# Three w_out loads and the loads of steps 6 and 7 change places in one DMA queue of an mLSTM + MLP kernel, with the conversion of w_out later and half of the key/query copies on VectorE

## The chip, the cores and the metric

The kernel runs on 1 core of one Trainium2 chip. Its time is the device time of one execution in microseconds (us). Before the change it is 527.63 us, the median of 3 runs (525.84 to 529.88). The profile is one further execution of 524.4 us, whose recorded span is 522.5 us; 1.9 us lie around the span. All times of day below are microseconds from the start of that span.

## The reference

Two blocks follow each other. The first is an mLSTM cell over 4 batches, 8 heads, 768 positions and head size 40:

```python
for t in range(S):
    m_new = np.maximum(f_gate[:, :, t] + m, i_gate[:, :, t])
    ...
    C = f_stab * C + i_stab * np.einsum('bhd,bhe->bhde', vt, kt)
    n = f_stab * n + i_stab * kt
    h_tilde = np.einsum('bhde,bhe->bhd', C, qt)
    denom = np.maximum(np.abs(np.einsum('bhd,bhd->bh', n, qt)), 1.0)
    y[:, :, t] = sigmoid(o_gate) * h_tilde / denom
```

Its result, seen as 3072 tokens of 320 values, goes through an MLP: `h = x @ w_in` (320 to 2048), `g = max(0.01*h, h)`, `out = g @ w_out` (2048 to 320). The two weight matrices arrive as 8-byte floats; everything is computed in fp32.

## The kernel before

**Tiling.** The 768 positions are 6 chunks of 128. A step is one chunk of one batch, so steps 0 to 3 are chunk 0, steps 4 to 7 chunk 1, and so on to step 23. The MLP of chunk g is a list of "ff units", which the main loop runs in the pass c = g + 1, and between these units it puts the attention work of chunk c ("cells"). So the pass c = 1 holds the MLP of chunk 0 and the attention of steps 4 to 7. In this pass 30 units remain, numbered i = 0 to 29 in the loop: i = 0 to 13 are the first product in half tiles (`half`, TensorE L790, ScalarE's activation at L798), i = 14 to 29 are the second product (`part`, TensorE L825): 14 to 17 need rows of w_out pieces 0 and 1, 18 to 21 pieces 2 and 3, 22 to 25 pieces 4 and 5, 26 to 29 pieces 6 and 7.

**Order.** The instructions of TensorE, VectorE, ScalarE and GpSimd stand in the order in which the program writes them. The loads are issued by SP, one queue in order; their places among each other come out of the scheduler, which sets an issue later when what it overwrites is still in use. In the built program every SP transfer also waits for the one eight places before it in the queue.

**A step of chunk 1** has these parts. Loads: `load` brings k into `kn` (L380) and v in four pieces into `S` (L383); `spread` brings the decay row into `w` (L437, two transfers from the kernel's own scratch `a_dr`); both together are `feed(s)`. `load_late(s, 1)` brings q into `rb` (L406), called from `ahead(s - 2)`; `load_late(s, 2)` the output gate. GpSimd adds the mask to w (L479), scales q into `y` (L517), k into `vu` (L508), and the state (L622). `u_split` turns k and q with 64 small matmuls into two PSUM banks (L564, "tk"), each of which then holds k of one half step and q of the other, and four copies bring them to `kqT` (L570). `u_parts` first splits the scaled q (L550 "tq", copies at L552), then makes scores and state update (L644 and L649, "sd"); ScalarE makes the exponentials of w (L488, eight per step, handed out between other work), VectorE multiplies them with the scores into `qn` (L654). `u_plain` makes the outputs (L695, "hN").

The cells of steps 4, 5, 6 and 7 stand behind fixed units: `u_parts` behind i = 2, 7, 12 and 18, `u_plain` behind i = 5, 10, 15 and 21. `u_split(s + 1)` comes right behind `u_plain(s)`.

**Weights.** Pieces of 8-byte floats are loaded by `load_weights` (w_in at L222, w_out at L229, eight w_out pieces of 640 KB) and converted by `narrow_weights`: ScalarE L243, ScalarE L245, VectorE L247, ScalarE L251, VectorE L253, VectorE L257. The generator `now` hands these six steps out, so many per unit: first the last two pieces of w_in (12 steps, done at i = 7 before and after the change), then w_out pieces 0 to 7 (48 steps).

Of the kernel before, what the change touches and what calls it, by code (L numbers as in the profile page):

```python
# [21 lines left out]
def kernel(  # L22
# [26 lines left out]
    nc = tc.nc  # L49
    B, H, S, D = q.shape  # L50
# [12 lines left out]
    SL = P // 2  # L63
# [30 lines left out]
    def load_fi(c):  # L94
        t = fi[c] = wk.tile([BH, 2, P], F32, name="fi")
        eng = nc.scalar if c < 3 else nc.sync
        eng.dma_start(t[:, 0, :], f_all[:, ts(c, P)])
        eng.dma_start(t[:, 1, :], i_all[:, ts(c, P)])
# [65 lines left out]
    QN = NF // 4  # L164
# [20 lines left out]
    def run_of(r, at):  # L185

        ks = SLOTS[r][at:]
        return ks[0], next((i for i in range(1, len(ks)) if ks[i] != ks[i - 1] + 2), len(ks))

    def load_weights(n, halves=(0, 1)):  # L190

        m = n - QN
        if n < QN:
            dst = w_in[:, n, :]
        else:
            dst = w_out[:, 2 * m : 2 * m + 2, :].rearrange("p a d -> p (a d)")
        to = dst
        if wide:
            if n < 2:
                at = NF * GT - 2 * WC * (n + 1)  # L200
                raw = acts_l[:, at : at + 2 * WC].bitcast(U64)
            elif n < QN:
                raw = raw_t[:, WC * (n - 2) : WC * (n - 1)]
            elif m < 2:
                raw = w_out[:].rearrange("p f d -> p (f d)")[:, (2 + m) * WC : (3 + m) * WC].bitcast(U64)
            else:
                at = (4, 0, 1, 2, 3, 4)[m - 2] * HW
                raw = raw_t[:, at : at + HW]
            raws[n] = (raw, dst)
            to = raw  # L210
        if n < QN:
            src = moe_w_in[:, n * QC : (n + 1) * QC].rearrange("(k p) (r c) -> r p k c", p=DP, r=2)
            by_slot = to.rearrange("p (k c) -> p k c", k=KC)
            by_half = to.rearrange("p (e k c) -> p e k c", e=2, c=P)
            for r in halves:
                at = 0
                while at < KC:
                    k0, many = run_of(r, at)
                    rows, ks = slice(DP * r, DP * (r + 1)), slice(k0, k0 + 2 * many - 1, 2)
                    eng = nc.gpsimd if r and n < 3 else nc.sync  # L220
                    if wide or n > 1:
                        eng.dma_start(by_slot[rows, at : at + many, :], src[r, :, ks, :])  # L222
                    else:
                        for e in range(2):
                            eng.dma_start(by_half[rows, e, at : at + many, :], src[r, :, ks, e * P : (e + 1) * P])
                    at += many
        else:
            rows = moe_w_out[2 * m * P : 2 * (m + 1) * P, :]
            nc.sync.dma_start(to.rearrange("p (a d) -> p a d", d=Dm), rows.rearrange("(a p) d -> p a d", p=P))  # L229
# [166 lines left out]
    def natural(s, i):  # L396

        t = rb_t[s % NR][:, i]
        return t[:, : H * D].rearrange("p (h d) -> p h d", d=D)
# [154 lines left out]
    def u_split(s):  # L554

        d = st[s]
        d["kqT"] = wk.tile([P, 2, PR * P], F32, name="kqT")
        src = (d["k"], natural(s, 1))
        bank = [psc.tile([P, H, SL], F32, name=f"tk{r}", tag="c") for r in range(2)]
        for h in range(H):  # L560
            for i in range(2):
                for u, toks, rows in subs(s):
                    out_rows = rows if i == 0 else slice(SL * u, SL * u + D)
                    nc.tensor.matmul(  # L564
                        bank[u][out_rows, h, :], lhsT=src[i][toks, h, :D], rhs=ident[toks, toks], start=True, stop=True,
                    )
        for i in range(2):
            for u, toks, rows in subs(s):
                out_rows = rows if i == 0 else slice(SL * u, SL * u + D)
                nc.scalar.copy(d["kqT"][rows, i].rearrange("p (h t) -> p h t", t=SL), bank[u][out_rows])  # L570

    def u_transpose(s, copy=nc.scalar.copy):
        d = st[s]
# [289 lines left out]
    def run(steps, n=None):  # L863

        for _ in range(H if n is None else n):
            next(steps, None)

    def ahead(s):

        if s < NS:  # L870
            if s < 2 * B:
                u_split(s)
            if s >= 2 * B:
                late[s] = 3
            lazy[s] = prep_exp(s)
            if s < 2 * B:
                prep_qs(s)
            else:
                prep_kq(s)
            if s + NR < NS:  # L880
                load_late(s + NR, 0)
                load_late(s + NR, 1)
                if s + NR >= 2 * B:
                    spread_q(s + NR)
            state_next(s, 0)
            prep_vu(s)
            if s + 1 <= 2 * B:
                prep_mask(s + 1)

    def feed(s):  # L890
        load(s)
        spread(s)
# [96 lines left out]
    with tc.manual_schedule(engines={E.PE, E.DVE, E.Activation, E.Pool}):  # L989
        ffs, part = first_chunk()  # L990
        for s in (B, B + 1):
            load_late(s, 1)
            feed(s)
            load_late(s, 2)
            load_weights(s - B + 2)
        for n in range(3):
            load_weights(QN + n)
        for s in (B + 2, B + 3):
            feed(s)


        ffs = ffs[2:]
        fetch = {5: (3, 4), 8: (5, 6), 15: (7,)}
        place = (2, 5, 7, 10, 12, 15, 16, 18, 21, 22, 24, 26, 28)
        late = {}
        masks = {0: (2, 3), 12: (4, 5)}
        pairs = (2, 2, 6, 6, 14, 14, 19, 19, 19)
        now = (None for n in range(2, QN + NF // 2) for _ in narrow_weights(n))
        for c in range(1, NB + 1):
            if c > 1:  # L1010
                ffs = ff_units(c - 1)
            cells = cell_units(c) if c < NB else []
            n_ff, n_c = len(ffs), len(cells)
            done = fed = 0
            waiting = []
            for i in range(n_ff):
                if c == 1:
                    run(now, (0, 0, 0, 3, 3, 0)[i] if i < 6 else 3 if i < 14 else 4)
                    for n in fetch.get(i, ()):
                        load_weights(QN + n)  # L1020
                for s, steps in lazy.items():
                    if s in late and late[s] > 0:
                        late[s] -= 1
                    else:
                        run(steps, 3)
                for n in masks.get(i, ()) if 1 < c < NB else ():
                    if c * B + n < NS:
                        prep_mask(c * B + n)
                ffs[i]()
                if c == 1 and i == 0:  # L1030
                    run(part)
                    prep_mask(B)
                    ahead(B)
                    load_fi(3)
                if c + 1 < NB:
                    if i == (1 if c == 1 else 0):
                        gates(c + 1)
                    if i == (3 if c == 1 else 2):
                        gates_exp(c + 1)
                upto = min(n_c, sum(p <= i for p in (place if c == 1 else pairs)))  # L1040
                while done < upto:
                    fn, s = cells[done]
                    fn(s)
                    done += 1
                    if fn is u_mix:
                        waiting.append(s)
                    if fn is u_plain and s < 2 * B - 1 or fn is u_parts and s == 2 * B - 1:
                        ahead(s + 1)
                    elif fn is u_mix:
                        ahead(s + 2)  # L1050
                    elif fn is u_plain:
                        prep_mask(s + 2)
                        ahead(s + 2)
                if i >= n_ff // 2 - 1:
                    for s in waiting:
                        gather_x(s)
                    waiting.clear()
                while fed < done:
                    fn, s = cells[fed]
                    fed += 1  # L1060
                    if fn in (u_mix, u_plain):
                        load_late(s + NR, 2)
                        if s + NL < NS:
                            feed(s + NL)
# [31 lines left out]
```

## Time and profile before

| | PE | DVE (VectorE) | ACT (ScalarE) | POOL (GpSimd) |
|---|---|---|---|---|
| busy us of the 522.5 us span | 509.1 | 205.3 | 187.6 | 106.9 |
| share of the span | 97% | 39% | 36% | 20% |

Time of the profiled execution: 524.4 us; its span: 522.5 us; mean granted TensorE clock 0.992. In the page, PE is TensorE's matmuls, SP the engine that issues the loads. Over the span the chain of work that ended last lies 89% on PE, 5% on SP's queue and 2% on transfers. From 90 us to the end of the last product TensorE is busy without a gap that the profile shows.

By lines, TensorE spends 216.5 us in the first product (L790) and 211.1 us in the second (L825). Of the waits of TensorE's matmuls the longest single one is the one for `rb<-in_q_dram` in L564: 2.9 us. The SP queue carries 56.31 MB in 163408 packets, most of them under 512 bytes.

### The profile page before, as it was taken

To read this page: it belongs to the slowest core of one execution; us is meant where nothing else is said; L and a number is where in the kernel's file an instruction comes from. 1 tells how busy PE (TensorE), PEld (TensorE's weight loads), DVE (VectorE), ACT (ScalarE), POOL (GpSimd) and SP (SyncE) were. 2 spreads that over 40 slices of the span, in tenths; PEclk is the share of its full clock that TensorE was granted. 3 is DMA by queue.
4 is the path that set the end of the run, shared out by engine and by line. 5 is a ranking of instruction groups with operands and counts; after the bars stand their busy time and mean duration, and the time that the engine had idled before them with its cause. 6 is when DMAs were issued, how large, how long until landed. Compare 5 with 4: busy or idle time off the path is not lost.

```text
span 522.5 us, 11302 instructions
## 1 busy us (share of the span) xinstructions
PE 509.1 (97%) x4507; PEld 331.1 (63%) x4507; DVE 205.3 (39%) x400; ACT 187.6 (36%) x477; POOL 106.9 (20%) x149
## 2 busy tenths in 40 slices
PE   8989987999999999999999999999999999999997
PEld 6878876777554677554677554677554677544674
DVE  6666453767048264048264038253037240000000
ACT  5559896858425122125112125112125100122100
POOL 4363313424015031016021016021013010000000
PEclk9889999999999999999999999999999999999999
DMA  9999875989646535665536665625532112000000
GB/s 122 137 206 156 180 188 145 220 196 169 159 92 135 127 80 148 141 140 125 123 93 155 139 140 116 134 82 157 136 77 71 44 40 87 14 0 1 13 13 25
DMA packets 164419, 59.12 MB, mean 113 GB/s; under 512 B 128432, under 2 KB 155632, under 8 KB 164368
## 3 DMA queue, kind: packets, MB, share of 16 engines
q1 hardware_dynamic: 163408, 56.31, 50.1%
q0 software_dynamic: 576, 1.97, 2.0%
q8 instruction: 35, 0.57, 0.5%
q10 hardware_dynamic: 384, 0.13, 0.1%
q14 instruction: 16, 0.13, 0.1%
HBM read 51.68 MB, written 6.70 MB: 112 GB/s over the span
## 4 chain that ended last, share of the span: by engine, by line
PE 89%; SPq 5%; DMA 2%; ACT 2%; issue 1%; DVE 1%; ACTq 0%; DVEq 0%
PE po L825 40%; PE ph L790 39%; SPq L378 3%; PE pT L725 3%; PE sd L644 3%; DMA acts<-in_moe_w_in_dram 1%; PE sd L649 1%; PE tk L564 1%; PE hN L695 1%; DMA rb<-in_q_dram 1%; PE tq L550 1%; SPq L383 0%; SPq L392 0%; ACT kqT L570 0%; PE tg L357 0%
## 5 line engine op out<-in xcount | busy, mean ns | idle before, releaser
L790 PE MATMUL ph<-xT,w_in 64*128 64x512 f32 (+1 forms) x1120 | 216.5, 537 | 3.5 <-ACT acts L798 1.9
L825 PE MATMUL po<-w_out,acts 128*128 128x320 f32 x768 | 211.1, 434 | 0.0
L825 PEld LDWEIGHTS po<-w_out,acts 128*128 128x128 f32 x768 | 144.5, 190 | 62.6 <-issue 3.8
L790 PEld LDWEIGHTS ph<-xT,w_in 64*128 64x128 f32 x1120 | 108.6, 189 | 97.5 <-issue 87.7
L798 ACT ACTIVATE acts<-ph 128x512 f32<-128x512 f32 (+1 forms) x112 | 53.6, 531 | 141.5 <-PE ph L790 141.5
L654 DVE TENSOR_TENSOR qn<-w,sd 64x512 f32<-64x512 f32 x40 | 27.4, 684 | 106.7 <-PE sd L649 58.6
L479 POOL TENSOR_TENSOR w<-w,i 128x512 f32<-128x512 f32 x20 | 27.3, 1375 | 126.0 <-DMA w<-a_dr 74.0
L622 POOL TENSOR_TENSOR S<-S,f 40x336 f32<-40x336 f32 x36 | 28.0, 779 | 102.1 <-PE pT L725 65.2
L488 ACT ACTIVATE w<-w,gT 128x64 f32<-128x64 f32 x160 | 41.2, 338 | 0.0
L833 ACT COPY y<-po 128x320 f32<-128x320 f32 x12 | 5.1, 422 | 83.2 <-PE po L825 83.2
L833 ACT COPY hn<-po 128x320 f32<-128x320 f32 x12 | 5.1, 425 | 75.7 <-PE po L825 75.7
L541 DVE TENSOR_TENSOR qn<-kqT,ea 64x512 f32<-64x512 f32 x32 | 26.9, 840 | 0.9
L732 DVE STREAM_TRANSPOSE hb<-pT 128x512 f32<-128x512 f32 x16 | 11.4, 714 | 39.2 <-PE pT L725 39.0
L739 POOL TENSOR_TENSOR xb<-xb,den 128x320 f32<-128x320 f32 x16 | 11.6, 727 | 67.1 <-DVE xb L736 67.1
L644 PEld LDWEIGHTS sd<-kqT 40*64 40x64 f32 x640 | 19.9, 135 | 6.1 <-issue 6.1
L644 PE MATMUL sd<-kqT 40*64 40x64 f32 x640 | 21.6, 220 | 0.0
L535 DVE STREAM_TRANSPOSE kqT<-rb 128x512 f32<-128x512 f32 x32 | 20.7, 686 | 1.2 <-DMA rb<-in_q_dram 1.1
L743 DVE STREAM_TRANSPOSE x<-xb 128x512 f32<-128x512 f32 x16 | 18.1, 1132 | 7.7 <-POOL xb L739 7.7
L649 PE MATMUL sd<-S,vu 64*40 64x42 f32 x576 | 20.2, 214 | 0.7 <-issue 0.7
L649 PEld LDWEIGHTS sd<-S,vu 64*40 64x40 f32 x576 | 18.6, 111 | 0.9 <-issue 0.9
L626 DVE TENSOR_TENSOR S<-S,sd 40x336 f32<-40x336 f32 x36 | 18.1, 503 | 1.0
L725 PEld LDWEIGHTS pT<-qn,S 128*64 128x64 f32 x512 | 15.6, 138 | 3.6 <-issue 3.5
(138 smaller groups left out, 348.9 us busy)
## 6 DMA issues: line engine op xcount, KB each, us to landing
w<-a_dr SPq DMA_DIRECT2D x40, 128.0 KB
rb<-in_k_dram SPq DMA_DIRECT2D x64, 80.0 KB
rb<-in_q_dram SPq DMA_DIRECT2D x64, 80.0 KB
rb<-in_o_gate_dram SPq DMA_DIRECT2D x64, 80.0 KB
ea<-a_dr SPq DMA_DIRECT2D x32, 128.0 KB
kn<-in_k_dram SPq DMA_DIRECT2D x24, 160.0 KB
raw<-in_moe_w_out_dram SPq DMA_DIRECT2D x6, 640.0 KB
S<-in_v_dram SPq DMA_DIRECT2D x80, 40.0 KB
```

The costliest lines, as they stand in the source:

```text
L479: nc.gpsimd.tensor_tensor(w, w, cm2.unsqueeze(1).to_broadcast([P, H, SL]), op=ALU.add)
L488: yield nc.scalar.activation(w[:, h, :], of, AF.Exp, bias=gT[c][:, 0, bh : bh + 1], scale=1.0)
L535: nc.vector.transpose(d["kqT"][:, i].rearrange("p (h t n) -> p h n t", n=TS, t=QW), raw_blocks(s, i, QW).rearrange("p (h n) d -> p h n d", ...
L541: nc.vector.tensor_tensor(mixed(s)[rows, 1 - r], d["kqT"][rows, 1].rearrange("p (h t) -> p h t", t=SL), d["ea"][rows], op=ALU.mult,)
L622: nc.gpsimd.tensor_tensor(new, old, g, op=ALU.mult)
L644: nc.tensor.matmul(bank[1 - u][toks, h, :], lhsT=kqT[rows, 0, ts(h, SL)], rhs=kqT[rows, 1, ts(h, SL)], start=True, stop=True,)
L649: nc.tensor.matmul(dC[u][:, h].rearrange("p k d -> p (k d)"), lhsT=d["ku"][toks, h], rhs=S_v[s % NL][toks, u, h, :, :V1], start=True, stop ...
L654: nc.vector.tensor_tensor(mixed(s)[toks, u], w[toks], bank[1 - u][toks], op=ALU.mult)
L725: nc.tensor.matmul(pT[DP * r : DP * (r + 1), j * P + u * SL : j * P + (u + 1) * SL], lhsT=S[:, u, h, :], rhs=m[:, u, h, :], start=True, st ...
L790: nc.tensor.matmul(ph[r][:, cols], lhsT=w_row(r, slot, j), rhs=xT[DP * r : DP * (r + 1), slot, cols], start=(slot == 0), stop=(slot == KC ...
L798: nc.scalar.activation(acts[:, f, cols], ph[r][:, cols], AF.Prelu, alpha=0.01)
L825: nc.tensor.matmul(po[n][:], lhsT=acts[:, f, ts(n, P)], rhs=w_out[:, f, :], start=(f == 0), stop=(f == NF - 1),)
```

## The change

```diff
@@ u_split
-                nc.scalar.copy(d["kqT"][rows, i].rearrange("p (h t) -> p h t", t=SL), bank[u][out_rows])
+                (nc.vector.tensor_copy if i else nc.scalar.copy)(
+                    d["kqT"][rows, i].rearrange("p (h t) -> p h t", t=SL), bank[u][out_rows],
+                )
@@ before the main loop
             load_weights(s - B + 2)
-        for n in range(3):
-            load_weights(QN + n)
-        for s in (B + 2, B + 3):
-            feed(s)
...
-        fetch = {5: (3, 4), 8: (5, 6), 15: (7,)}
+        fetch = {2: (0, 1, 2), 7: (3, 4), 10: (5, 6), 15: (7,)}
@@ in the main loop
-                    run(now, (0, 0, 0, 3, 3, 0)[i] if i < 6 else 3 if i < 14 else 4)
+                    run(now, (0, 0, 0, 3, 3, 0, 3, 3, 0, 0)[i] if i < 10 else 3 if i < 14 else 4)
...
                     prep_mask(B)
                     ahead(B)
+                    feed(B + 2)
                     load_fi(3)
...
+                if c == 1 and i == 5:
+                    feed(B + 3)
```

Of the four copies of `u_split`, the two of k stay on ScalarE and the two of q go to VectorE, for steps 4 to 7. Units 8 and 9 hand out no conversion step, so w_out's pieces 0 and 1 are converted in units 10 to 13 (before: 8 to 11) and pieces 2 to 7 in units 14 to 22 (before: 12 to 21). The order on TensorE is unchanged. On SP, the two built programs differ from the last w_in transfer on, up to k of step 8 (numbers are pieces or steps, x the number of transfers):

```
before: w_out 0, 1, 2 | k6, v6 x4, w6 x2 | k7, v7 x4, w7 x2 | q6 | gates x2 | a_dr | gates x2 | k8
after:  k6, v6 x4, w6 x2 | gates x2 | w_out 0 | q6 | w_out 1, 2 | a_dr | gates x2 | k7, v7 x4, w7 x2 | k8
```

The same 23 transfers stand in front of k8 in both. Behind it the order is that of before, but for w_out pieces 5 and 6, which stand one transfer earlier. In VectorE's order the two copies of q stand behind the last state addition of the step before, and each waits for ScalarE's copy out of the same PSUM bank. Piece 1's L253 and L257 stand behind the score products L654 of step 6, and piece 7's three steps behind the transposes of step 9 (before: in front of step 7's outputs).

## The prediction

> **What bounds the kernel now.** I read the busy time by stretches first, to see where TensorE has gaps at all.
>
> ```profile
> core 0: us, PE busy (x) PEld busy (x) DVE busy (x) ACT busy (x) POOL busy (x), PEclk, DMA share, GB/s
> ...
> 40.00:60.00 20.00, 19.25 (x301) 16.26 (x297) 11.10 (x21) 19.18 (x41) 5.34 (x5) 1.00 0.88 149
> 60.00:70.00 10.00, 9.27 (x237) 8.18 (x238) 4.45 (x8) 8.49 (x17) 3.75 (x5) 1.00 1.07 293
> 70.00:80.00 10.00, 8.72 (x96) 7.32 (x92) 6.78 (x10) 9.81 (x22) 1.51 (x2) 1.00 0.58 91
> 80.00:90.00 10.00, 7.25 (x191) 6.43 (x194) 3.10 (x7) 6.02 (x13) 4.69 (x6) 1.00 0.53 124
> 90.00:100.00 10.00, 10.00 (x155) 7.58 (x147) 6.29 (x13) 9.37 (x21) 1.10 (x2) 1.00 1.02 214
> ```
>
> From 40 to 90 TensorE lacks 0.75 + 0.73 + 1.28 + 2.75 = 5.5 us. The change starts behind 44 us, and from 90 on PE is full, so 5.5 us is all that it can win; a wait that it makes behind 90 costs its whole length. TensorE's timeline names the gaps:
>
> ```profile
> 57.40 2.69 PE L790 MATMUL ph<-xT,w_in 64*128 64x256 f32 x20 [0.75 <-ACT acts L798]
> ...
> 75.87 2.70 PE L790 MATMUL ph<-xT,w_in 64*128 64x256 f32 x20 [1.12 <-ACT acts L798]
> ...
> 82.75 0.25 PE L564 MATMUL tk<-ident,rb 64*40 64x64 f32 x2 [2.88 <-DMA rb<-in_q_dram]
> ```
>
> Two are waits for ScalarE to empty PSUM (units 5 and 10), the largest is q of step 6. The remaining 0.73 us (at 68.69, in step 5's scores) is put down to issue, and I count nothing for it. The chain of waits shows what follows:
>
> ```profile
> 79.62 3.10 DMA rb<-in_q_dram
> 82.75 1.09 PE tk L564 x60
> ...
> 92.68 4.50 PE po L825 x16
> 97.18 1.06 PE hN L695 x32
> 98.24 1.12 PE tk L564 x64
> ```
>
> q6 needs 3.1 us from issue to use; unit 14 starts at 92.68; step 7's tk at 98.24. SP's queue says why q6 is issued so late:
>
> ```profile
> 58.84 1.12 SPq L229 DMA_DIRECT2D w_out<-in_moe_w_out_dram  x2
> ...
> 61.02 11.76 SPq L383 DMA_DIRECT2D S<-in_v_dram  x4
> ...
> 79.62 0.53 SPq L406 DMA_DIRECT2D rb<-in_q_dram  x1
> ...
> 94.33 0.56 SPq L406 DMA_DIRECT2D rb<-in_q_dram  x1
> ```
>
> v6 is held up for 11.76 us behind three w_out pieces. The last line is q7: 94.33 + 3.10 = 97.4, only 0.8 us before its use. ScalarE:
>
> ```profile
> 65.13 1.38 ACT L243 ACTIVATE w_in<-raw 128x1280 f32<-128x1280 f32 x1 [0.53 <-DMA raw<-in_moe_w_in_dram]
> ...
> 73.87 0.77 ACT L243 ACTIVATE w_out<-w_out 128x640 f32<-128x640 f32 x1
> 74.67 0.92 ACT L245 ACTIVATE w_out<-w_out 128x640 uint16<-128x640 uint32 x1
> 75.46 0.63 ACT L798 ACTIVATE acts<-ph 128x256 f32<-128x256 f32 x2
> ...
> 83.88 2.36 ACT L570 COPY kqT<-tk 40x512 f32<-40x512 f32 x4 [3.97 <-PE tk L564]
> ```
>
> **q copies on VectorE.** ScalarE loses two of four copies, 2 x 0.58 = 1.16 us per step (2.36 for four). VectorE gains two; its nearest row is L581's copy of 128x512 out of PSUM, 671 ns, so 1.34 us. In step 4 this frees ScalarE early enough (L798 at 57.00 becomes 55.8, before TensorE's 56.6) that the 0.75 us wait goes. It is given back: ScalarE then waits for the last w_in piece, which is in front of all moved loads and starts L243 at 65.13 as before; everything queued behind that up to unit 6's L798 (68.89) stays, and unit 8, which started at 69.54, needs it. Gain 0 to 0.1; I take 0. On VectorE the copies delay the gate scan (3.2 us from 48.65) by 1.3 us; L654 behind it ran at 54.27 waiting for ScalarE, which is now 1.16 us earlier, so nobody is later than before.
>
> The row of L570 gives four copies one after the other, 2.36 us; in the built program VectorE's copy waits for ScalarE's out of the same bank, so the four end after 0.58 + 2 x 0.67 = 1.9 us instead of 1.25 if they ran side by side. The Trainium skill (PSUM — Partial Sum Buffer, "PSUM bank collisions raise a hardware error") has two engines on one bank kept apart by a wait per bank, or per bank and quadrant of 32 partitions; k and q lie in different quadrants here, so its finer rule would allow the 1.25. Nobody waits for the 0.65 us: step 6's scores come 5.5 us behind tk.
>
> **Conversion later.** L243 and L245 leave the place in front of unit 8's L798, which then runs at 73.87 instead of 75.46. Unit 9 ends at 74.6, so unit 10 starts there and not at 75.87: gain 1.2 us. (w_out 0 is now converted from 75 on; see its landing below.)
>
> **q6.** In front of q6 stand k6, v6, w6, two small gate loads and w_out 0. If v6 kept its whole 11.76 us, q6 would be issued at 58.84 + 0.45 + 11.76 + 1.2 + 0.9 + 0.55 = 73.7 and land at 76.8. It is needed when tk of step 6 starts: 74.6 plus 2.6 (unit 10) plus 1.06 (hN) = 78.3. So even in the worst case it is in time; the cover is 1.5 us, likely 5 (v6 has lost the three pieces in front of it). Gain 2.9 us. w6's mask add (L479, which ran at 76.88) only gets earlier.
>
> **What is late next.** From 75.87 to 92.68 TensorE has 16.8 us less 2.88 of wait, 13.9 of work. Unit 14 would start at 74.6 + 13.9 = 88.5, that is 4.2 us early. But pieces 0 and 1 are then only just converted. tk of step 6 ends at 79.7; behind it ScalarE has two copies (1.16), L251 (0.8), three and three and two exponentials (0.73, 0.73, 0.5), two L798 pairs (0.55 each), L243 and L245 (1.7), two L552 copies (1.1): 7.8 us, so w of step 6 is ready at 87.6. VectorE's L654 and L626 take 1.9, then piece 1's L253 and L257 0.5 + 0.83: ready at 90.8. Unit 14 does two of its four f-rows before it needs piece 1 (1.1 us, to 89.6) and waits 1.2 us. The bounds are 0 (ScalarE 1.2 us quicker) and 2.5 (each ScalarE row a fifth longer, and GpSimd slowing VectorE: L257 is seen at 1.86 us beside a mask add). I take 1.2. TensorE is then 3.0 us ahead.
>
> tk of step 7 would so start at 95.2, and q7 must have landed. Its issue moves with the queue. At the low end not at all: 23 transfers stand in front of k8 either way, and the 1.92 MB of w_out, 6.6 us at the 293 GB/s of 60:70, only moved behind step 6. Then q7 lands at 97.4, and 0.8 us of the gain is left. At the other end: the issues in front of k8 took 23.9 us (58.84 to 82.73) and would take some 14 us unblocked, 10 less, and the DMA share from 70 to 90 is 0.58 and 0.53. v7, now behind w_out 1 and 2, will be held as v6 was. I take 2 us, nearer to no shift, because each blocked issue must see transfers land that also move: q7 at 95.4, a wait of 0.2 us, gain left 2.8. Halfway regard for the low end gives 2.4.
>
> Pieces 2 and 3 (unit 18): piece 3's last steps stand behind the copies of step 7, so they are ready at q7 plus tk, two copies, L251, L257 (0.1 + 1.2 + 0.9 + 0.8 = 3 us) while TensorE needs 5.2 us (L825 2.25, gate matmuls 0.7, L825 2.25) from the same point: 2 us of cover wherever q7 lies. Piece 7 stands behind step 9's transposes: with its q at the old 122.5 it is ready at 122.5 + 1.3 + 1.9 + 1.8 = 127.5, needed at 128.53 + 1.1 - 2.4 = 127.2. Between 0.3 us of wait and 2 us of cover; I take 0.
>
> **Sum.** 1.2 + 2.9 - 1.2 = 2.9, cut by q7 to 2.4. Span 522.5 - 2.4 = 520.1. The profiled execution (524.4) is 3.2 us under the median, so I carry the difference: 527.63 - 2.4 = 525.2.
>
> **A new wait and the clock.** The granted clock is 0.84 in 20:40, where TensorE has long gaps, and 1.00 in 80:90 in spite of the 2.88 us wait. The Trainium skill (TensorE: Matmul & The Clock Gate, "What's actually happening") halves the clock after an idle window of about 3.4 us. By it a wait for q7 longer than that would cost some 1.7 us more, as an estimate from that page; the sum has no such wait and goes without it.
>
> **Rivals.** (1) No new wait: piece 1 and q7 are in time. For it: ScalarE has slack from 60 to 90; against: L654 stands in front of piece 1. Gain 4.2: 523.4. (2) The queue is no earlier: q7 lands at 97.4, tk of step 7 waits 2.2 us, gain 0.8: 526.8. For it: the same bytes and issues. Against: the half-empty DMA from 70 to 90. (3) Slower: w_out's conversion falls behind TensorE. Each group of second-product units starts with a wait for its piece; at 1.5 to 2 us in each of the four groups, 6 to 8 us go and 4.2 come: about 530. It decides from a lag of 1.05 us per group on average. Against it: 2 us of cover at unit 18 and more at unit 22. (4) The diff does not do what it says: in the built order q6 is not first but behind w_out 0 and k6, v6, w6. By the bound above this costs nothing, so it changes no number.
>
> **The numbers.** Forecast (gain 1.2 to 3.4) 0.55; (1) 0.16; (2) 0.17; (3) 0.12. About 1% (5.3 us) can be told from no change. Over 1% faster needs the whole 5.5 us, the end of (1): 0.05. Over 1% slower is the bad half of (3): 0.06. Same: 0.89. The range goes from (1) with a little more, 5 us, 522.6, to part of (3), 528.6.
>
> **What would show it.** Right: no wait for `rb<-in_q_dram` near 79; unit 10 starting at about 74.6; L798 right in front of L243 of w_out 0; a wait of about 1 us in the first L825 for VectorE's L257; q7 issued at about 92 and TensorE's tk of step 7 waiting for it or just not. Wrong: a new gap in L825 beyond 2 us, a q7 issue behind 94, or v7 held so long that w7 delays GpSimd's mask add in front of step 7's `y`.

## The result and the profile after

| | median | range | runs |
|---|---|---|---|
| before | 527.1 us | 524.6 to 529.9 | 20 |
| after | 529.8 us | 527.3 to 534.1 | 20 |

The ratio is 1.0054 (95% interval 1.0033 to 1.0075): 1.7 to 4.0 us slower, where 2.4 us faster was forecast. The profiled execution of the changed kernel took 532.3 us (span 530.5), 2.4 us above its median, while that of the kernel before was 2.7 us under its own. So the two spans stand 8.0 us apart, and sizes are taken from the repeated runs, not from this pair. In the code after, the lines named here that stand behind 570 are two higher (L825 is L827).

The busy time by stretches, after (columns as in the prediction):

```profile
core 0: us, PE busy (x) PEld busy (x) DVE busy (x) ACT busy (x) POOL busy (x), PEclk, DMA share, GB/s
...
70.00:80.00 10.00, 8.42 (x107) 7.49 (x106) 5.54 (x7) 9.91 (x23) 1.27 (x1) 1.00 0.78 230
80.00:90.00 10.00, 10.00 (x246) 8.91 (x247) 5.03 (x10) 8.53 (x23) 5.05 (x6) 1.00 0.85 145
90.00:100.00 10.00, 7.10 (x62) 4.62 (x58) 5.35 (x11) 5.71 (x9) 0.76 (x1) 1.00 0.92 191
100.00:110.00 10.00, 9.04 (x107) 6.45 (x108) 7.93 (x12) 6.88 (x14) 6.11 (x7) 1.00 0.99 250
...
120.00:130.00 10.00, 7.08 (x24) 4.60 (x23) 8.15 (x16) 4.88 (x12) 2.33 (x4) 0.83 0.98 174
130.00:140.00 10.00, 9.65 (x40) 6.67 (x39) 6.11 (x12) 7.31 (x26) 3.40 (x3) 1.00 0.75 175
```

The stretch from 80 to 90, which lacked 2.75 us, is full: the wait for q6 is gone. But from 90 on, where TensorE had no gap before, it now lacks 2.90 + 0.96 + 2.92 + 0.35 = 7.1 us, and in 120:130 the granted clock is 0.83. The waits of TensorE after (in total, times, longest) name what it waits for:

```profile
PE po L827 <- DVE w_out L257: 4.3, 3, 2.9
...
PE tk L564 <- DMA rb<-in_q_dram: 2.8, 1, 2.8
...
PE ph L792 <- ACT acts L800: 0.9, 1, 0.9
```

The first row is three waits for w_out pieces in the second product, the second is q of step 7. TensorE's timeline gives their places:

```profile
93.38 3.50 PE L827 MATMUL po<-w_out,acts 128*128 128x320 f32 x12 [1.08 <-DVE w_out L257]
...
100.96 0.25 PE L564 MATMUL tk<-ident,rb 64*40 64x64 f32 x2 [2.78 <-DMA rb<-in_q_dram]
...
123.46 2.50 PE L827 MATMUL po<-w_out,acts 128*128 128x320 f32 x4 [2.92 <-DVE w_out L257]
...
134.85 1.34 PE L827 MATMUL po<-w_out,acts 128*128 128x320 f32 x4 [0.35 <-DVE w_out L257]
```

In this order: piece 1 (unit 14), q7 (tk of step 7), piece 5 (unit 22), piece 7 (unit 26). VectorE's timeline, after, says why pieces 5 and 7 are late:

```profile
119.11 0.71 DVE L535 STREAM_TRANSPOSE kqT<-rb 128x512 f32<-128x512 f32 x1 [4.84 <-DMA rb<-in_q_dram]
119.86 1.54 DVE L541 TENSOR_TENSOR qn<-kqT,ea 64x512 f32<-64x512 f32 x2
121.43 0.49 DVE L247 TENSOR_SCALAR w_out<-w_out 128x640 f32<-128x640 f32 x1
121.96 0.49 DVE L253 TENSOR_SCALAR w_out<-w_out 128x640 uint32<-128x640 uint32 x1
122.58 0.83 DVE L257 CUSTOM_DVE_ANT_0 w_out<-w_out,raw 128x1280 uint16<-128x1280 uint16 x1
...
128.18 1.30 DVE L535 STREAM_TRANSPOSE kqT<-rb 128x512 f32<-128x512 f32 x2
129.52 1.91 DVE L541 TENSOR_TENSOR qn<-kqT,ea 64x512 f32<-64x512 f32 x2
131.45 0.90 DVE L247 TENSOR_SCALAR w_out<-w_out 128x640 f32<-128x640 f32 x1
132.39 1.45 DVE L253 TENSOR_SCALAR w_out<-w_out 128x640 uint32<-128x640 uint32 x1
133.97 0.82 DVE L257 CUSTOM_DVE_ANT_0 w_out<-w_out,raw 128x1280 uint16<-128x1280 uint16 x1
```

The three steps at 121.43 are piece 5: they stand behind the transposes of step 8 (L535), and VectorE waited 4.84 us there for q8. The three at 131.45 are piece 7, behind those of step 9. Before the change neither was so:

```profile
107.14 0.83 DVE L257 CUSTOM_DVE_ANT_0 w_out<-w_out,raw 128x1280 uint16<-128x1280 uint16 x1
109.74 1.40 DVE L654 TENSOR_TENSOR qn<-w,sd 64x512 f32<-64x512 f32 x2 [1.77 <-ACT w L488]
...
122.61 0.82 DVE L257 CUSTOM_DVE_ANT_0 w_out<-w_out,raw 128x1280 uint16<-128x1280 uint16 x1 [0.89 <-DMA rb<-in_q_dram]
...
124.87 1.31 DVE L535 STREAM_TRANSPOSE kqT<-rb 128x512 f32<-128x512 f32 x2
```

Piece 5 was done at 107.97, in front of step 7's score products, and piece 7 at 123.43, in front of step 9's transposes (124.87). With the later conversion the six steps of each piece are handed out one or two units later, and pieces 5 and 7 cross a wait for a load. The two parts of the order that the text before the prediction names (pieces 1 and 7) were not all: piece 5 moved too.

### The profile page after: what moved, and what is told of

Its sections match the earlier page's. It is cut to its first block, busy times and chain, and to the rows that moved or that the text cites. A ratio compares the mean times of both kernels' runs of the same rounds, so it can differ in the third digit from the quotient of the medians.

```text
span 530.5 us, 11292 instructions
## 1 busy us (share of the span) xinstructions
PE 510.4 (96%) x4507; PEld 331.4 (62%) x4507; DVE 210.5 (40%) x408; ACT 183.3 (35%) x469; POOL 107.1 (20%) x149
## 4 chain that ended last, share of the span: by engine, by line
PE 77%; SPq 12%; DMA 5%; ACT 2%; DVE 2%; issue 1%; POOL 0%; DVEq 0%; ACTq 0%; POOLq 0%
PE ph L792 35%; PE po L827 34%; SPq L383 3%; SPq L378 3%; PE pT L727 3%; DMA raw<-in_moe_w_out_dram 2%; PE sd L646 2%; SPq L222 2%; DMA raw<-in_moe_w_in_dram 1%; SPq L437 1%; PE sd L651 1%; SPq L392 1%; ACT w L488 1%; SPq L380 1%; DMA rb<-in_o_gate_dram 1%
## 5 line engine op out<-in xcount | busy, mean ns | idle before, releaser
L827 PE MATMUL po<-w_out,acts 128*128 128x320 f32 x768 | 213.2, 436 | 4.3 <-DVE w_out L257 4.3
L827 PEld LDWEIGHTS po<-w_out,acts 128*128 128x128 f32 x768 | 144.9, 191 | 68.2 <-DVE w_out L257 5.9
L800 ACT ACTIVATE acts<-ph 128x512 f32<-128x512 f32 (+1 forms) x112 | 53.6, 530 | 141.0 <-PE ph L792 140.9
L535 DVE STREAM_TRANSPOSE kqT<-rb 128x512 f32<-128x512 f32 x32 | 20.6, 683 | 4.9 <-DMA rb<-in_q_dram 4.8
```

The lines of the kernel that those rows point to most:

```text
L535: nc.vector.transpose(d["kqT"][:, i].rearrange("p (h t n) -> p h n t", n=TS, t=QW), raw_blocks(s, i, QW).rearrange("p (h n) d -> p h n d", ...
L800: nc.scalar.activation(acts[:, f, cols], ph[r][:, cols], AF.Prelu, alpha=0.01)
L827: nc.tensor.matmul(po[n][:], lhsT=acts[:, f, ts(n, P)], rhs=w_out[:, f, :], start=(f == 0), stop=(f == NF - 1),)
```

## The experiments

All ratios are to the kernel before on the same chip, with their 95% intervals.

| kernel | ratio | interval | median us |
|---|---|---|---|
| changed, once more | 1.0058 | 1.0033 to 1.0084 | 529.6 |
| changed, pieces 5 and 7 early | 0.9964 | 0.9940 to 0.9988 | 524.7 |
| changed, only piece 5 early | 1.0080 | 1.0052 to 1.0107 | 531.9 |
| changed, only piece 7 early | 1.0017 | 0.9991 to 1.0042 | 528.6 |
| changed, conversion as before | 0.9977 | 0.9956 to 0.9997 | 525.5 |
| before + later conversion | 1.0074 | 1.0046 to 1.0103 | 531.6 |
| before + new loads | 0.9976 | 0.9950 to 1.0002 | 526.5 |
| before + copies on VectorE | 0.9992 | 0.9968 to 1.0016 | 527.2 |
| changed, four steps from unit 10 | 0.9970 | 0.9939 to 1.0001 | 526.4 |
| the same, q7 by ScalarE's queue | 1.0385 | 1.0348 to 1.0421 | 548.2 |
| the same, q7 by GpSimd's queue | 0.9929 | 0.9910 to 0.9947 | 523.5 |
| q7 by GpSimd's queue, other deal of steps | 0.9930 | 0.9900 to 0.9959 | 523.6 |

**The changed kernel once more.** No edit.

> The changed kernel once more, for a second profile. Theory A (the time goes in waits that the order of the program makes): the same gaps of TensorE stand again, about 1.1 us in the first products of L827 for piece 1, 2.8 us for q of step 7, 2.9 us in L827 for piece 5, and the time is 2 to 4 us above the kernel before. Theory B (what was seen is the disturbance of one execution, whose loads were already 3 us late at 56 us, in front of everything that the change moves): the last w_in load is issued at 56 us as before, q of step 7 lands by 98 us, and the wait for it is under 1 us.

Theory A. The same waits stand again: 1.08 us for piece 1, 2.60 for q7, and for pieces 5 and 7 now 0.35 and 2.48. Theory B asked for the last group of w_in loads at 56 us, and it came late again, at 59.08 (59.29 in the first profile), so these two profiles alone do not separate the theories. Others below do. With piece 7 early the group is issued at 56.67, and 2.92 us are still waited for piece 5; with the new loads alone it is issued at 59.48, and no piece is waited for. So that lateness does not make the waits. Pieces 5 and 7 share one lead of TensorE: what is not waited for at the one is waited for at the other.

**Pieces 5 and 7 early.**

```diff
-  run(now, (0, 0, 0, 3, 3, 0, 3, 3, 0, 0)[i] if i < 10 else 3 if i < 14 else 4)
+  run(now, (0, 0, 0, 3, 3, 0, 3, 3, 0, 0)[i] if i < 10 else 3 if i < 14 else {16: 5, 17: 5, 18: 6}.get(i, 4))
```

> Only the conversion steps of units 16, 17 and 18 are changed, to 5, 5 and 6, so that piece 5 stands in front of the products of step 7 and of the transposes of step 8 on VectorE, as it did before the change. Theory A: the wait of 2.9 us in L827 for L257 goes, and the time falls by 2 to 3 us against the changed kernel, to about that of the kernel before (ratio 0.998 to 1.002). Theory B: the wait only moves to the next late load, and the ratio stays at 1.004 to 1.007.

4.9 us under the changed kernel (529.6 to 524.7), more than theory A's 2 to 3. The edit does one thing that the expectation does not name: all 48 steps are handed out by unit 21, so piece 7 stands in front of step 9's transposes again, too. TensorE's waits from 90 on:

```profile
PE tk L564 <- DMA rb<-in_q_dram: 2.1, 1, 2.1
PE po L827 <- DVE w_out L257: 1.1, 1, 1.1
```

Those for pieces 5 and 7 are gone; q7 and piece 1 are left. Part of the 4.9 us is the clock: its mean over the runs is 0.9880 in the changed kernel (8 runs) and 0.9917 here (12 runs), which is at most 2.0 us by estimate (the difference times the span). The two pieces were then moved one by one.

**Only piece 5, only piece 7.** The entry for late units becomes

```diff
@@ only piece 5 early
+  {16: 5, 17: 5, 18: 6, 19: 3, 20: 3, 21: 2}.get(i, 4)
@@ only piece 7 early
+  {19: 5, 20: 5, 21: 6}.get(i, 4)
```

> The changed kernel with piece 5 in front of step 7's products and step 8's transposes, and piece 7 left behind step 9's transposes. Theory A: TensorE, no longer held by piece 5, reaches piece 7 earlier and waits 2 to 3 us for it; ratio 1.000 to 1.004. Rival (piece 5 is the whole cost): ratio 0.994 to 0.998, as with both early.

> The changed kernel with 5, 5 and 6 conversion steps in units 19, 20 and 21: piece 7 comes in front of the transposes of step 9 again, piece 5 stays behind those of step 8. Theory A (both pieces cost, whichever gap TensorE meets first): the wait for piece 5 stays at 0.4 to 3 us, that for piece 7 goes; ratio 1.000 to 1.004. Rival (piece 5 is the whole cost): ratio 1.004 to 1.007 as the changed kernel.

With piece 5 alone nothing is won: 1.0080 is above the ranges of both theories. TensorE's waits from 90 on are one row with two of them, 1.1 us for piece 1 and 4.6 for piece 7:

```profile
PE po L827 <- DVE w_out L257: 5.7, 2, 4.6
```

The wait is longer than the 2 to 3 us of theory A, and in 130:140 of this profile the granted clock is 0.66, another 3.4 us. With piece 7 alone the ratio is 1.0017, and 2.92 us are waited for piece 5. So each is a wall by itself, piece 7 the higher one, and only both together give the 4.9 us. The rival that piece 5 is the whole cost is out.

**The parts of the change, each alone.** In the changed kernel the deal of the conversion steps is undone, then the copies too, which leaves the new loads alone. In the kernel before, the later conversion alone and the copies alone are done, as in the diff of the change.

```diff
@@ changed kernel, conversion as before
-  run(now, (0, 0, 0, 3, 3, 0, 3, 3, 0, 0)[i] if i < 10 else 3 if i < 14 else 4)
+  run(now, (0, 0, 0, 3, 3, 0)[i] if i < 6 else 3 if i < 14 else 4)
@@ changed kernel, loads alone: that, and
-  (nc.vector.tensor_copy if i else nc.scalar.copy)(
+  nc.scalar.copy(
```

> The changed kernel with the conversion steps handed out as before the change (w_out 0 in units 8 and 9). Theory A: the waits for pieces 1 and 5 go (4 us), but ScalarE now waits for w_out 0, which lands at 77.7 us, in front of unit 8's L800, and TensorE waits some 2 to 3 us in unit 10; sum 1 to 2 us below the changed kernel. Theory B: the conversion is not what costs, so the new wait in unit 10 is added and the time is 2 us above the changed kernel.

> The kernel before with only the later conversion. Theory A: unit 10's wait of 1.1 us goes, but is spent in the wait for q of step 6, which lands as before; piece 5 then stands behind the transposes of step 8, done at 115.6 us, and is ready at 117.5 us, 0.5 us after the second product needs it: 0 to 1.5 us slower than before. Theory B: within 0.5 us of before.

> The kernel before with the new order of the loads alone; conversion and copies as before. The later conversion cost 0.74% by itself, and the changed kernel without it stood at 0.9977. Theory A: the loads win what they can, q of step 6 (2.9 us), but pay with ScalarE's wait for w_out 0 in unit 8 (2 us in unit 10), so 0.5 to 2 us faster than before (ratio 0.996 to 0.999). Rival: the gain of the changed kernel without the later conversion came from the copies on VectorE, and the loads alone are at 0.999 to 1.002.

> The kernel before with the two q copies on VectorE alone. Theory A: ScalarE gets 1.16 us back per step, at most the 0.75 us wait of unit 5 and part of unit 10's 1.1 us go, and the wait for q of step 6 takes them: ratio 0.998 to 1.001. Rival: the copies carry the gain, 0.996 to 0.998.

The later conversion costs 0.74% by itself and 0.81% within the change (1.0058 over 0.9977), so the whole loss is its. On the kernel before it cost 3.9 us, more than the 0 to 1.5 expected, and at other pieces: its profile waits 0.85 us for piece 1 and 2.13 for piece 7, and not for piece 5. The clock does not explain the rest: its mean is 0.989 in these 9 runs and in the 28 of the kernel before on the same chip. Undoing the later conversion in the changed kernel wins 4.1 us, where theory A had 1 to 2. The new loads alone stand at 0.9976, with an interval that just reaches 1; the copies alone cannot be told from nothing. In the profile of the loads alone TensorE's longest wait is one of 2.9 us for ScalarE's L800:

```profile
PE ph L792 <- ACT acts L800: 2.9, 1, 2.9
PE tk L564 <- DMA rb<-in_q_dram: 1.6, 1, 1.6
```

This is not the price that theory A named. ScalarE's timeline shows what it waited for:

```profile
69.84 1.38 ACT L243 ACTIVATE w_in<-raw 128x1280 f32<-128x1280 f32 x1 [3.83 <-DMA raw<-in_moe_w_in_dram]
...
78.57 0.78 ACT L243 ACTIVATE w_out<-w_out 128x640 f32<-128x640 f32 x1
```

It is the last piece of w_in, in front of unit 6's L800, which unit 8 needs; w_out 0 is met at 78.57 without a wait. With the conversion as before it is the same: 5.00 us of ScalarE for w_in, 2.02 of TensorE in unit 8, and none for w_out 0.

**Piece 1's wait.** Four steps in every unit from 10 on, so that pieces 0 and 1 stand in front of step 6's score products.

```diff
-  ... if i < 10 else 3 if i < 14 else 4)
+  ... if i < 10 else 4)
```

> The changed kernel with four conversion steps in every unit from 10 on, so that pieces 0 and 1 are handed out before the cell of step 6 and piece 5 before that of step 7. Theory A: against the changed kernel the waits for pieces 1, 5 and 7 all go (1.1, 2.9 and 0.4 us, and the lower clock behind the longest); TensorE still waits 2 to 3 us for q of step 7. Time 523 to 525 us, ratio 0.993 to 0.997. Rival: piece 1's wait was covering that for q of step 7, which now grows by as much, and the time is that of the kernel with piece 5 early (0.9964).

The rival holds. No wait for L257 is left from 90 on, but the one for q7 is 3.7 us where it was 2.1, and the ratio (0.9970) is that with piece 1 waiting (0.9964). The ratio alone, with its interval from 0.9939 to 1.0001, would not tell the theories apart; the wait does.

```profile
PE tk L564 <- DMA rb<-in_q_dram: 3.7, 1, 3.7
```

**q7 out of SP's queue.** The kernel with four steps from unit 10, and `load_late(7, 1)` replaced, first on ScalarE, then on GpSimd:

```diff
@@ ahead(6), in front of state_next: ScalarE's queue
+  nc.scalar.dma_start(natural(7, 1), q[7 % B, :, ts(1, P), :].rearrange("h p d -> p h d"))
@@ ahead(6), behind prep_vu: GpSimd's queue
+  nc.gpsimd.dma_start(natural(7, 1), q[7 % B, :, ts(1, P), :].rearrange("h p d -> p h d"))
```

> As the kernel with four steps from unit 10, and q of step 7 is asked for by ScalarE's own queue behind the copies of step 6 (about 80 us) in place of SP. Theory A: the 2 to 3 us wait of tk of step 7 goes whole, and nothing is close behind: 2 to 3 us faster than without (ratio 0.988 to 0.992). Rival: the wait is given back by the next group of second products or by q of step 8, which stands in SP's queue behind the same loads, and less than 1 us is won.

> As the kernel with four steps from unit 10, with q of step 7 asked for by GpSimd in place of SP, behind its vu of step 6 (about 84 us). GpSimd's own queue shares no semaphore with SP's loads: the instruction waits for nothing. Theory A: it lands by 95 us, the wait of 3.7 us in tk of step 7 goes whole and nothing is close behind; ratio 0.988 to 0.992. Rival: the wait is given back by the next late load (q of step 8 stands in SP's queue behind the same loads), less than 1 us is won, ratio 0.995 to 0.998.

The first went wrong in another way than either theory said. ScalarE stood still for 27.21 us with the issue at its head:

```profile
108.43 0.40 ACTq L887 DMA_DIRECT2D rb<-in_q_dram  x1
108.88 0.77 ACT L243 ACTIVATE w_out<-w_out 128x640 f32<-128x640 f32 x1 [27.21 <-DMA S<-in_v_dram]
```

In the built program this issue waits for one of the eight completion semaphores (the counters by which a transfer reports that it has landed) that SP's loads use in turn, and the profile names a later v load as what released it. So it says nothing of q7. GpSimd's issue has a semaphore of its own: there the wait for q7 is gone and 0.4% is won (0.9970 to 0.9929), on two chips and with intervals that overlap. That lies between the two theories: the 3.7 us are in part given back. The mean clock of the runs is 0.9879 with SP's issue (12 runs) and 0.9928 with GpSimd's (6 runs), at most 2.6 us by the same estimate, so most of what is won can be the clock. The largest wait of the pass from 90 on is then 1.8 us of the gate transposes for step 6's outputs, which on VectorE stand behind piece 3.

**Another deal of the steps.** q7 by GpSimd, and

```diff
-  run(now, (0, 0, 0, 3, 3, 0, 3, 3, 0, 0)[i] if i < 10 else 4)
+  run(now, (0, 0, 0, 3, 3, 0, 3, 3, 0, 0, 4, 4, 4, 0, 4, 4, 5, 5, 6)[i] if i < 19 else 4)
```

> As the kernel with q of step 7 in GpSimd's queue, but with the conversion dealt out so that no piece stands in front of what TensorE needs: four steps in units 10 to 12, none in 13, four in 14 and 15, then 5, 5, 6, so that piece 3, whose load ends at about 95 us, comes behind step 6's outputs and not in front of them. Theory A: the wait of 1.8 us of the gate transposes for step 6's outputs goes (and the clock's 1.7 us behind it): ratio 0.988 to 0.992. Rival: the late load of piece 3 is then met at unit 18, and the ratio stays at 0.992 to 0.995.

The rival: 0.9930. The gate transposes still wait 1.1 us, unit 18 now waits 1.2 us for piece 3, and 1.05 us at 134.75 are waited for ScalarE's copies of xT (L777). Both versions with q7 by GpSimd are 0.7% faster than the kernel before and 1.3% faster than the changed one.

## Why the prediction was wrong, point by point

**What held.** Unit 10's wait and q6's wait are gone (q6 is issued at 72.59, lands at 78.9 and is needed at 81.1; issue to landing is 6.3 us where 3.1 were taken, and the cover paid for it). From the start of unit 6 to that of unit 14 TensorE takes 26.9 us after (64.02 to 90.95) and 30.5 before (62.12 to 92.61): 3.6 us won where 4.2 were reckoned; a wait of 0.88 us of unit 8 for ScalarE was not in that sum. (Unit 9 ended at 74.75 before, 75.87 less 1.12, and not at 74.6.) Piece 1's wait is 1.08 us, 1.2 were taken. The copies on VectorE neither cost nor win anything that can be told.

**The last w_in piece.** The prediction took ScalarE's start on the last w_in piece as unmoved, because its load is in front of all moved loads. But L243 starts 9.1 to 10.4 us after the issue of that group in the eleven profiles with the new loads, and 8.9 us after it in two of the three with the old (in the third nothing waits for it). Unit 8 waits 0.26 to 2.92 us in ten of the eleven and in none of the three. Why the piece lands later is not shown.

**q7.** It was taken at 95.4, with a wait of 0.2 us; it was used at 101.0 and 101.1 in the two profiles, after 2.78 and 2.60 us. The step "I take 2 us, nearer to no shift" was wrong, and its low end right. Before the change q7 was issued at 94.33, 38.1 us behind the start of the last w_in group:

```profile
56.20 2.60 SPq L222 DMA_DIRECT2D raw<-in_moe_w_in_dram  x4
```

After it:

```profile
59.29 2.60 SPq L222 DMA_DIRECT2D raw<-in_moe_w_in_dram  x4
...
97.41 1.22 SPq L406 DMA_DIRECT2D rb<-in_q_dram  x1
```

That is again 38.1 us. Over all kernels where SP issues q7 it is 37.9 in the two others with the old order and 37.3 to 38.7 in the eight with the new one. The order of the 23 transfers changes nothing in when the queue is through. This is the mechanism of rival (2). The issues of v6, which took 11.76 us behind three w_out pieces, still take 7.0 us (62.57 to 69.60) with none of them in front, and those of v7, now behind w_out 1 and 2, take 5.5 where they took 3.15. In the working itself, "halfway" between the gains of 2.8 and 0.8 is 1.8, not 2.4; the forecast would have been 525.8.

**Pieces 5 and 7, the step that failed.** The prediction took piece 7 as "Between 0.3 us of wait and 2 us of cover; I take 0", and gave unit 22 (piece 5) "more" than 2 us of cover without a sum. Measured: 0.35 to 2.9 us at piece 5, 0.35 to 4.6 at piece 7, and 4.9 us in the runs for both. For piece 7 the working put the start of step 9's transposes at 122.5, the landing of q9 of before; already in the trace before they start at 124.87. Two waits stand in front of them that the working left out. After:

```profile
125.04 0.78 ACT L243 ACTIVATE w_out<-raw 128x640 f32<-128x640 f32 x1 [8.79 <-DMA raw<-in_moe_w_out_dram]
125.85 0.93 ACT L245 ACTIVATE raw<-raw 128x640 uint16<-128x640 uint32 x1
126.64 0.44 ACT L524 ACTIVATE rb<-rb 128x320 f32<-128x320 f32 x1
```

Piece 7's load, issued at 118.89 (before: 114.45; 3.1 of these 4.4 us stood at the last w_in group already), is met by ScalarE in front of step 7's gate (L524); VectorE's outputs of step 7 wait for that, and the transposes of step 9 for VectorE: they start at 128.2, not 122.5, and piece 7 is ready at 134.8. Piece 5 was not seen at all: the text before the prediction named pieces 1 and 7 as moved on VectorE, while every piece had slid back. The trace before would have given it: there step 8's transposes and the products behind them end at 115.6, the three steps of piece 5 make that 117.4, and unit 22 starts at 116.51 and wants the piece 1.1 us later, by the forecast 2.4 us earlier still: by estimate a wait of some 2 us.

In the first profile the 3.6 us won stand against 7.1 us of waits from 90 us on, 3.5 us slower; the repeated runs have 2.7. Two signs of being wrong that the prediction had named came: a gap in L825 beyond 2 us (2.92) and a q7 issue behind 94 (97.41).

**The rivals.** Rival (3), the slower one, had the right mechanism, w_out's conversion too late for the second product, and about the right time (530). Its shape was wrong: not every group of units pays, but those whose piece has slid behind a wait for a load.

**The clock.** The sum took a wait at its length. A single wait can cost more, as the last section shows: 1.7 us in each of the two profiles after. But the kernel before has such falls too (0.84 in 20:40 of its profile), and the mean clock of the runs is 0.989 before (28 runs) and 0.989 and 0.988 after (20 and 8 runs). So the clock is no visible part of the loss.

## What to carry to other kernels

When a stream of small steps is dealt out later in an in-order engine, list for every one of its items the first instruction that it has slid behind, and price those that themselves wait for a load; a slide by one slot is harmless until it crosses one. Changing the order in a full queue brings one load forward by putting others back (q6 was issued 23.4 us behind the last w_in group before, 13.3 after), and leaves the time at which the queue is through. A load that keeps the same transfers in front of it comes earlier only by leaving the queue, and the engine that then issues it must not share a completion semaphore with the queue. A gap on the bound engine is priced at its length, and a fall of the clock behind it can add to that.

## What was not expected of the hardware

Late in gaps of TensorE or just behind them the granted clock falls to one half for 3.4 or 6.8 us. The busy time by stretches of 2 us in the first profile after, around the wait for piece 5:

```profile
120.00:122.00 2.00, 0.54 (x3) 0.03 (x1) 1.92 (x4) 0.00 (x0) 0.15 (x1) 1.00 0.87 162
122.00:124.00 2.00, 0.54 (x1) 0.50 (x2) 1.84 (x4) 0.00 (x0) 0.00 (x0) 0.78 1.24 275
124.00:126.00 2.00, 2.00 (x6) 1.14 (x5) 1.60 (x5) 0.93 (x2) 0.00 (x0) 0.50 1.28 147
126.00:128.00 2.00, 2.00 (x9) 1.56 (x8) 0.85 (x2) 2.00 (x5) 0.25 (x1) 0.86 0.78 168
```

The loss is (0.22 + 0.50 + 0.14) x 2 = 1.7 us, and the four matmuls at 123.46 take 2.50 us where four take 1.34 at 134.85. Of the 15 gaps of 2.0 to 4.6 us between 40 and 150 in eleven of the profiles (that with 27 us of ScalarE left out), 10 were followed by it: five lost 1.7 us, five 3.4. Five were not, among them the 2.88 us of the kernel before and 3.1 us with the copies alone, while 2.02 and 2.11 us were. Four more falls stand at or behind gaps of 0.7 to 1.9 us. The Trainium skill (TensorE: Matmul & The Clock Gate, "What's actually happening") has the clock halved after an idle window of about 3.4 us, the windows running freely. The stretches of 3.4 and 6.8 us agree with that length; that gaps of 2.0 to 2.9 us were enough does not agree with a whole idle window, and the measurement decides. Whether the phase of the windows picks the gaps no run here shows.
